# Window attention with a normalised feed-forward block: the largest weight is spread behind the first second product, in another bank, and GpSimd makes the weights' three low bits

## The chip, the core and the metric

The kernel runs on one core of one Trainium2 chip. A core has a matrix engine (TensorE, "PE" in the rows, its weight loads "PEld"), VectorE ("DVE"), ScalarE ("ACT"), GpSimd ("POOL") and a sync engine ("SP") whose queue issues every DMA of this kernel. Matmuls write into banks of PSUM; the other tiles lie in SBUF. The metric is the device time of one execution in microseconds (us); lower is better.

## The reference

Eight batches of 576 tokens with eight heads of 64 go through attention with a window of 64 keys, and the 4608 tokens of 512 numbers that come out go through a feed-forward block. Cut to what matters:

```python
scores = where(0 <= row - col < 64, (q @ k.T) / 8, -1e6)   # per batch and head
x = softmax(scores) @ v                      # 4608 x 512, heads side by side
h = x @ w_in                                 # first product, 512 -> 1024
e = exp(h - max(h)); sm = e / (sum(e) + 1e-9)
solu = h * sm
ln = (solu - mean(solu)) / sqrt(var(solu) + 1e-6) * g_ln
return ln @ w_out                            # second product, 1024 -> 512
```

The two weights come as 64-bit floats; the kernel turns them into 32-bit floats on the chip.

## The kernel before

**Tiles.** The 4608 tokens are 36 tiles of 128. Tile t is scored (`pS`, L491), its softmax rows `sS` are exponentiated on ScalarE (L528) and divided by their sums (`rec`, L540, then L544), turned (bank `t`, copied out as `PT`, L603) and multiplied with the values (`pX`, L622). The result `xH` (and from tile 3 on its rest `xL`) goes through the first product into `pH` (L650 for tiles 0 to 2, in full 32-bit; L661 from tile 3 on, three passes over split weights). `moe_norm` reads `pH` twice on VectorE (the maximum, L676, and the product with the exponentials, L681) and leaves the normalised rows `e` (L700). `pH` has one buffer, so the first product of a tile waits for L681 of the tile before.

**The second product.** It runs three tiles behind. Tile 0 is turned on TensorE (L756), multiplied with the gains into `yT` (ScalarE L764 for columns 0 to 3, VectorE L765 for 4 to 7) and multiplied in full 32-bit with the weights as they are (`pO`, L784). From tile 1 on the rows are split into two 16-bit planes `pl`, written to memory (`yd`, L737), read back turned (`yT`, L740) and multiplied with the split weights `w_outH` and `w_outL` in three passes (L794).

**Weights.** Eight blocks of 1 MB: 0 to 3 are `w_in`, 4 to 7 `w_out`. Of each, `raw` holds 1024 pairs (low word, high word) on a partition. ScalarE takes the magnitude of the high word (L353), VectorE clamps it (L355), shifts it (L358), puts sign and top bit back (L360) and adds the top three bits of the low word (L362). For blocks 4 to 7 the clamp also leaves each partition's largest value in `bound`.

**The largest weight.** `out_scale` turns `bound` into one scale for the split weights: small VectorE steps (L376 to L387) make a diagonal tile, one matmul with ones (L389) spreads it over all partitions, L391 takes the maximum, and L392 to L398 make the gains `gs_sb`, after which L425, L426 and L428 split `w_out`. The matmul writes into `pO_filler`, which shares its one PSUM buffer with the second product's `pO`; filler matmuls that only keep TensorE busy (L901) write there too. So L784 of tile 0 can't start before L391 has read.

**The order.** Every step is entered into a plan with an engine and a cost; the plan sorts all of them, and each engine runs its own list in that order and waits where it has to. `PLACES` says where tiles 2 to 5 are attended, `HOMES` which engine does a movable step, `RINGS` how many buffers a tile name has, `SCALED` in which round `out_scale` is entered.

Of the kernel before, what the change touches and what calls it, by code (L numbers as in the profile page):

```python
# [45 lines left out]
HOMES = {
    ("scale", 0, 0): "POOL", ("scale", 0, 1): "POOL", ("scale", 1, 0): "POOL", ("scale", 1, 1): "ACT",
    ("scale", 3, 0): "DVE", ("scale", 3, 1): "DVE", ("scale", 4, 0): "ACT", ("scale", 4, 1): "DVE",
    ("scale", 5, 0): "ACT", ("scale", 6, 1): "DVE", ("scale", 7, 1): "DVE", ("scale", 8, 0): "DVE",
    ("scale", 9, 0): "DVE", ("scale", 10, 0): "ACT",  # L50
    ("PT", 1, 0): "DVE", ("PT", 1, 1): "DVE", ("PT", 3, 0): "DVE", ("PT", 4, 1): "ACT", ("PT", 5, 1): "ACT",
    ("PT", 6, 1): "ACT",
    ("join", 4, 0): "DVE", ("join", 5, 1): "ACT", ("join", 7, 0): "ACT", ("join", 7, 1): "ACT",
    ("soft", 8, 0): "ACT", ("soft", 10, 0): "DVE",
    ("norm", 0, 0): "DVE", ("norm", 0, 1): "DVE", ("norm", 2, 0): "DVE", ("norm", 2, 1): "DVE",
    ("norm", 3, 0): "DVE",
    ("high planes", 1, 0): "DVE", ("high planes", 1, 1): "DVE", ("high planes", 2, 1): "DVE",
    ("high planes", 4, 0): "DVE", ("high planes", 6, 0): "DVE", ("high planes", 6, 1): "DVE",
    ("planes", 1, 1): "DVE", ("planes", 3, 1): "POOL", ("planes", 4, 0): "POOL", ("planes", 7, 0): "POOL",
    ("planes", 8, 0): "POOL",  # L60
    ("high", 0, 0): "POOL", ("high", 2, 0): "POOL", ("high", 2, 1): "POOL", ("high", 7, 0): "DVE",
    ("high", 7, 1): "POOL",
    ("split", 0, 1): "POOL", ("split", 2, 0): "POOL", ("split", 2, 1): "POOL", ("split", 3, 0): "POOL",
# [150 lines left out]
def tile_window_attention_solu_moe(  # L214
# [117 lines left out]
    def weight_block(i, src):  # L332
# [333 lines left out]
    def moe_norm(t):  # L666
# [284 lines left out]
```

## Time and profile before

| | us |
|---|---|
| median of 3 runs | 529.0 (528.93 to 529.11) |
| the profiled execution | 529.3 |
| its span, first to last instruction | 527.5 |
| TensorE busy in the span | 509.1 (97%) |
| VectorE, ScalarE, GpSimd busy | 363.5, 336.5, 256.4 |

The page counts a matmul as busy also where it stands at a lower clock, so the 97% is not 97% of the peak. All times in rows are from the span's start. A row of a timeline is: start, length, engine, line, operation, what it writes and reads, sizes, how many. Several instructions in a row are merged, so a length over many is that of all of them. "PEclk" is the granted TensorE clock: 1.00 is 2.4 GHz, 0.50 is 1.2 GHz.

### The profile page before, as it was taken

The page shows a single profiled execution, that of the slowest core. Times are in us where ns is not written, and L with a number is a line of the kernel's source. Part 1 is how long each engine was busy: PE and PEld are TensorE (multiplying, and loading weights), DVE is VectorE, ACT ScalarE, POOL GpSimd, SP SyncE. Part 2 cuts the span into 40 slices and gives each one's busy share as a digit, 9 for nine tenths or more (in the row PEclk, how much of TensorE's full clock was granted, in tenths as well). Part 3 has the DMA queues.
Part 4 walks back from the last instruction along what each step waited for, and adds up shares of the span by engine and source line. Part 5 has one row for each costly group of instructions (what it writes and reads, how often), then busy time and mean ns, then how long its engine had stood idle before and what let it go on. Part 6 is the DMA issues. An engine that isn't in the chain of part 4 may idle for free.

```text
span 527.5 us, 11422 instructions
## 1 busy us (share of the span) xinstructions
PE 509.1 (97%) x4238; PEld 339.3 (64%) x4238; DVE 363.5 (69%) x695; ACT 336.5 (64%) x968; POOL 256.4 (49%) x452
## 2 busy tenths in 40 slices
PE   8699985999999999999999999999999999999997
PEld 8566662676666666666666666666666666666653
DVE  4789996677677777777777777777777777745230
ACT  5458761778786666666666666666666666674240
POOL 5625551054466555555555555555555555562110
PEclk9799996999999999999999999999999999999999
DMA  8982243146899999999999899999999999699301
GB/s 347 418 315 92 68 132 108 49 147 217 250 251 251 262 251 247 260 258 251 248 250 250 245 252 264 267 252 252 248 246 231 264 248 260 190 236 206 101 24 56
DMA packets 157447, 115.56 MB, mean 219 GB/s; under 512 B 129872, under 2 KB 130128, under 8 KB 156880
## 3 DMA queue, kind: packets, MB, share of 16 engines
q1 hardware_dynamic: 157392, 114.84, 80.1%
q8 instruction: 33, 0.54, 0.4%
q14 instruction: 22, 0.18, 0.1%
HBM read 41.42 MB, written 41.42 MB: 157 GB/s over the span
## 4 chain that ended last, share of the span: by engine, by line
PE 89%; DVE 8%; POOL 1%; ACT 1%; issue 0%; POOLq 0%; ACTq 0%; DVEq 0%
PE pO L794 34%; PE pH L661 33%; PE pX L622 7%; PE pS L491 6%; PE pH L650 3%; PE pO L784 2%; PE pO_filler L901 1%; POOL sS L544 1%; PE pX L794 1%; PE t L598 1%; DVE w L360 1%; DVE w L362 1%; DVE mst L676 1%; DVE e L681 1%; DVE sS L544 1%; DVE w L355 1%
## 5 line engine op out<-in xcount | busy, mean ns | idle before, releaser
L794 PE MATMUL pO<-w_outH,yT 128*128 128x512 f16 x544 | 167.7, 380 | 0.0
L794 PEld LDWEIGHTS <-yT 128*128 128x128 f16 x840 | 79.6, 98 | 96.6 <-issue 5.1
L544 POOL TENSOR_SCALAR sS<-sS,rec 128x128 f32<-128x128 f32 x244 | 101.2, 436 | 83.2 <-DVE rec L540 51.7
L661 PE MATMUL pH<-w_inH,xH 128*128 128x512 f32 x264 | 110.4, 418 | 0.1
L528 ACT ACTIVATE sS<-sS,nmx 128x128 f32<-128x128 f32 x264 | 102.0, 389 | 7.5 <-DVE nmx L505 4.6
L661 PE MATMUL pH<-w_inH,xL 128*128 128x512 f32 x264 | 103.5, 392 | 0.8 <-DVE xL L633 0.8
L794 PE MATMUL pO<-w_outL,yT 128*128 128x512 f16 x272 | 103.1, 379 | 0.0
L661 PE MATMUL pH<-w,xH 128*128 128x512 f32 x264 | 101.6, 389 | 0.0
L676 DVE TENSOR_REDUCE mst<-pH 128x1 f32<-128x1024 f32 x36 | 44.1, 1224 | 60.6 <-PE pH L661 59.5
L731 DVE TENSOR_TENSOR pl<-e,pl 128x512 f16<-128x512 f32 x61 | 80.1, 1314 | 4.9 <-ACT pl L728 4.7
L694 POOL TENSOR_TENSOR mst<-mst,neghalf 128x1 f32<-128x1 f32 x36 | 20.4, 567 | 124.6 <-DVE mst L692 124.6
L805 ACT ACTIVATE ot<-pO,bound 128x512 f32<-128x512 f32 x34 | 23.4, 688 | 81.7 <-PE pO L794 72.6
L700 POOL TENSOR_SCALAR e<-e,mst 128x512 f32<-128x512 f32 x67 | 52.0, 783 | 20.7 <-DVE mst L695 20.2
L678 ACT ACTIVATE e<-pH,mst 128x1024 f32<-128x1024 f32 x36 | 40.2, 1117 | 29.4 <-DVE mst L676 28.4
L661 PEld LDWEIGHTS pH<-w_inH,xH 128*128 128x128 f32 x264 | 49.7, 188 | 13.0 <-issue 0.7
L661 PEld LDWEIGHTS pH<-w_inH,xL 128*128 128x128 f32 x264 | 49.4, 187 | 12.5 <-DVE xL L633 1.0
L661 PEld LDWEIGHTS pH<-w,xH 128*128 128x128 f32 x264 | 49.6, 188 | 10.5 <-issue 0.2
L564 POOL COPY raw<-sS 128x1024 uint16<-128x1024 uint16 x54 | 55.2, 1052 | 0.1
L687 ACT ACTIVATE pl<-e,mst 128x1024 bf16<-128x1024 f32 x36 | 41.4, 1149 | 15.8 <-DVE mst L684 14.3
L528 ACT ACTIVATION_READ_ACCUMULATOR sS<-sS,nmx 128x1 f32 x264 | 49.8, 189 | 0.0
L681 DVE CUSTOM_DVE_ANT_0 e<-pH,e 128x1024 f32<-128x1024 f32 x36 | 43.8, 1215 | 2.5 <-ACT e L678 2.5
L728 ACT CAST pl<-e 128x512 f16<-128x512 f32 x60 | 36.9, 617 | 5.3 <-POOL e L700 3.8
(117 smaller groups left out, 703.4 us busy)
## 6 DMA issues: line engine op xcount, KB each, us to landing
qk<-qk SPq DMA_DIRECT2D x36, 640.0 KB, 6.2
yd<-pl SPq DMA_DIRECT2D x33, 512.0 KB, 5.8
pd<-raw SPq DMA_DIRECT2D x28, 512.0 KB, 7.4
v<-vS SPq DMA_DIRECT2D x36, 256.0 KB, 4.2
y<-ot SPq DMA_DIRECT2D x35, 256.0 KB, 6.9
raw<-w_in SPq DMA_DIRECT2D x4, 1024.0 KB, 10.6
raw<-w_out SPq DMA_DIRECT2D x4, 1024.0 KB, 8.7
yT<-yd SPq DMA_TRANSPOSE x33, 5.3
```

Of the source, the lines that this page charges most:

```text
L528: plan.op("ACT", 580, lambda h=h: nc.scalar.activation(SS(t)[:, h], PS(t)[:, h // NPAIR, h % NPAIR] if t in MASKED else SS(t)[:, h], AF.Ex ...
L544: SS(t)[:, h], SS(t)[:, h], rec()[:, h:h + 1]) if e == "ACT" else units[e].tensor_scalar(
L564: plan.op(e, {"POOL": 1050, "ACT": 1000, "DVE": 700}[e], lambda x=x, e=e: copy_on(e)(PP(t)[:, :, 4 * x:4 * x + 4].rearrange("p k h n -> p ...
L622: nc.tensor.matmul(PX(t)[r * D:(r + 1) * D, p, ks], (V if half else VX)(t)[:, h * D:(h + 1) * D], PT(t)[:, r * NPAIR + p, ks], start=True, ...
L661: plan.op("PE", 233, lambda n=n, c=c, x=x, w=w: nc.tensor.matmul(PH(t)[:, hs], x(t)[:, c], w(c, h), start=(n == 0), stop=(n == len(passes) ...
L676: plan.op("DVE", 1230, lambda: nc.vector.tensor_reduce(nmax(), PH(t), axis=AX.X, op=ALU.max, negate=True), [("pH", t)], [key(0)])
L678: plan.op("ACT", 1320, lambda: nc.scalar.activation(E(t), PH(t), AF.Exp, bias=nmax(), scale=1.0, accum_out=se()), [("pH", t), key(0)], H2 ...
L681: plan.op("DVE", 1310, lambda: nc.vector.tensor_tensor_reduce(E(t), PH(t), E(t), scale=1.0, scalar=0.0, op0=ALU.mult, op1=ALU.add, accum_o ...
L687: plan.op("ACT", 1330, lambda: nc.scalar.activation(PL(t)[:, 0].bitcast(BF16), E(t), AF.Square, bias=nmean(), scale=1.0, accum_out=ss()), ...
L700: plan.op(e, {"POOL": 820, "DVE": 400}[e], lambda h=h, hs=hs, e=e: units[e].tensor_scalar(E(t)[:, hs], E(t)[:, hs], nmean(), kk(), ALU.add ...
L731: plan.op(e, {"POOL": 1450, "DVE": 690}[e], lambda hs=hs, e=e: units[e].tensor_sub(PL(t)[:, 1, hs], E(t)[:, hs], PL(t)[:, 0, hs]), [("e", ...
L794: plan.op("PE", 216, lambda f=f, i=i, x=x, k=k, y=y, w=w: nc.tensor.matmul(PO(), Y(t, y)[:, f], w(i, x), start=(f == k == 0), stop=(f == N ...
```

## The change

Parts, in the order of the diff:

- **Low bits.** ScalarE's magnitude is scaled by 2^-48, so the masks of L358 and L360 are not needed. A new step makes the three low bits of a block in place in `raw`: on GpSimd for seven blocks (a multiply and an add over 128x1024, read as unsigned integers), on VectorE for block 4. VectorE then has, for each block, the clamp and two two-input steps; the separate shift is gone, and the first two-input step waits for the new one.
- **`out_scale`.** Its matmul writes into a buffer of the transposes' bank `t`. It is entered after `moe_out` of round 3 and not before it, so it stands behind the second product of tile 0. One of its small steps goes.
- **First tile's rows** get a buffer `yF` of their own.
- **Square of `moe_norm`** writes into a tile `unread`, and no longer into the planes `pl` of its tile.
- **Tables.** Tile 4 is attended one place later, `PLANES` is 3, and `HOMES` puts other steps on other engines, among them four of tile 0's scalings on VectorE and most of the planes of tiles 2 to 5 on GpSimd.

```diff
+SHIFT = 2.0 ** -48
+LOW = 2.0 ** -29 * (1 - 2.0 ** -12)
-PLACES = {2: (0, 0), 3: (0, 2), 4: (1, 2), 5: (2, 2)}
+PLACES = {2: (0, 0), 3: (0, 2), 4: (1, 3), 5: (2, 2)}
-PLANES = 2
+PLANES = 3
 HOMES = {
-    ("scale", 0, 0): "POOL", ("scale", 0, 1): "POOL", ("scale", 1, 0): "POOL", ("scale", 1, 1): "ACT",
+    ("scale", 0, 1): "POOL", ("scale", 1, 0): "POOL", ("scale", 1, 1): "ACT", ("scale", 3, 0): "DVE",
...
+    ("low bits", 4, 0): "DVE",
...
-SCALED = 3
+SCALED = (3, 1)
...
+    unread = const.tile([P, DFF], BF16, name="unread")
...
-        plan.op("ACT", 1090, lambda: nc.scalar.activation(tf(), hi().bitcast(F32), AF.Abs), [R], [W])
+        plan.op("ACT", 1090, lambda: nc.scalar.activation(
+            tf(), hi().bitcast(F32), AF.Abs, scale=SHIFT), [R], [W])
+        e = home("low bits", i, 0, "POOL")
+        plan.op(e, {"POOL": 1900, "DVE": 700}[e], lambda: nc.gpsimd.tensor_scalar(
+            lo(), lo().bitcast(U32), LOW, 0.0018 - 0.5, ALU.mult, ALU.add) if e == "POOL" else nc.vector.tensor_scalar(
+            lo(), lo(), 29, 0, ALU.logical_shift_right, ALU.bitwise_or), [], [R])
...
-            tf(), tf(), EXP_HI, EXP_LO, ALU.min, ALU.max, accum_out=most), [W],
+            tf(), tf(), EXP_HI * SHIFT, EXP_LO * SHIFT, ALU.min, ALU.max, accum_out=most), [W],
-        plan.op("DVE", 700, lambda: nc.vector.tensor_scalar(
-            t(), t(), 0x07FFFFFF, 3, ALU.bitwise_and, ALU.logical_shift_left), [W], [W])
         plan.op("DVE", 1240, lambda: nc.vector.scalar_tensor_tensor(
-            t(), hi(), -0x40000000, t(), ALU.bitwise_and, ALU.bitwise_or), [R, W], [W])
+            t(), t(), 3, lo(), ALU.logical_shift_left, ALU.bitwise_or), [R, W], [W])
         plan.op("DVE", 1240, lambda: nc.vector.scalar_tensor_tensor(
-            t(), lo(), 29, t(), ALU.logical_shift_right, ALU.bitwise_or), [R, W], [W])
+            t(), hi(), -0x80000000, t(), ALU.bitwise_and, ALU.bitwise_or), [R, W], [W])
...
         def pM():
-            return T("pO", "filler", [P, DM], pool=ps_o)[:, P:2 * P]
+            return T("t", "most", [P, 4, P], pool=ps_t)[:, 0]
...
-            PL(t)[:, 0].bitcast(BF16), E(t), AF.Square, bias=nmean(), scale=1.0, accum_out=ss()),
-            H2 + [key(4)], [key(3), ("pl", t, 0), ("pl", t, 1)], lat=300)
+            unread, E(t), AF.Square, bias=nmean(), scale=1.0, accum_out=ss()),
+            H2 + [key(4)], [key(3)], lat=300)
...
-        return T("yT", t, [P, NF, P])
+        return T("yF" if t < PLAIN_OUT else "yT", t, [P, NF, P])
...
-            if t == SCALED:
+            if (t, 0) == SCALED:
                 out_scale()
...
             on(moe_out, t - BEHIND)
+            if (t, 1) == SCALED:
+                out_scale()
```

On TensorE, around the second product of tile 0 (`t_3` is the turning of tile 0's rows, `pS_6` the scores of tile 6, `pO_0` the second product, `pH_4` the first product of tile 4; the rows of `pX_4` are left out). Before:

```order
L756 MATMUL t_3_870<-ident_81,e_0_467 128x128 x4
L389 MATMUL pO_filler_173<-diag_123,ones_120 128x128
...
L901 MATMUL pO_filler_173<-ident_81 128x128 x4
L491 MATMUL pS_6_914<-qk_6_465 64x128 x16
L784 MATMUL pO_0_944<-w_4_510,yT_0_906 128x512 x2
L784 MATMUL pO_0_944<-w_5_521,yT_0_906 128x512 x2
L784 MATMUL pO_0_944<-w_6_639,yT_0_906 128x512 x2
L784 MATMUL pO_0_944<-w_7_648,yT_0_906 128x512 x2
L661 MATMUL pH_4_980<-w_inH_114,xH_4_942 128x512
```

And of the change:

```order
L764 MATMUL t_3_841<-ident_81,e_0_464 128x128 x4
...
L911 MATMUL pO_filler_174<-ident_81 128x128
L499 MATMUL pS_6_882<-qk_6_462 64x128 x16
L792 MATMUL pO_0_913<-w_4_509,yF_0_869 128x512 x2
L792 MATMUL pO_0_913<-w_5_516,yF_0_869 128x512 x2
L792 MATMUL pO_0_913<-w_6_621,yF_0_869 128x512 x2
L792 MATMUL pO_0_913<-w_7_633,yF_0_869 128x512 x2
L397 MATMUL t_most_954<-diag_124,ones_120 128x128
L669 MATMUL pH_4_957<-w_inH_114,xH_4_928 128x512
```

The spreading matmul stood ahead of `pO_0`, in its bank; now it stands behind it, in a bank of the transposes.

On VectorE at the same place (`w_6` and `w_7` are the last two weight blocks, `mst_3` and `e_3` the maximum and the exponentials' product of tile 3, `yT_0` or `yF_0` tile 0's turned rows, columns 4 to 7). Before:

```order
L358 TENSOR_SCALAR w_7_648<-w_7_648 128x1024
L360 SCALAR_TENSOR_TENSOR w_6_639<-raw_6_381,w_6_639 128x1024
L676 TENSOR_REDUCE mst_3_902<-pH_3_780 128x1
L362 SCALAR_TENSOR_TENSOR w_6_639<-raw_6_381,w_6_639 128x1024
L360 SCALAR_TENSOR_TENSOR w_7_648<-raw_7_412,w_7_648 128x1024
L765 TENSOR_SCALAR yT_0_906<-t_3_870,g_sb_117 128x128
L362 SCALAR_TENSOR_TENSOR w_7_648<-raw_7_412,w_7_648 128x1024
L765 TENSOR_SCALAR yT_0_906<-t_3_870,g_sb_117 128x128 x2
L681 ISA e_3_934,mst_3_902<-pH_3_780,e_3_934 128x1024
...
L519 SCALAR_TENSOR_TENSOR sS_6_960<-pS_6_914,maskNone_99 128x1024
...
L391 TENSOR_REDUCE bound_122<-pO_filler_173 128x1
```

And of the change:

```order
L371 SCALAR_TENSOR_TENSOR w_6_621<-w_6_621,raw_6_378 128x1024
...
L373 SCALAR_TENSOR_TENSOR w_6_621<-raw_6_378,w_6_621 128x1024
...
L371 SCALAR_TENSOR_TENSOR w_7_633<-w_7_633,raw_7_411 128x1024
...
L373 SCALAR_TENSOR_TENSOR w_7_633<-raw_7_411,w_7_633 128x1024
...
L684 TENSOR_REDUCE mst_3_846<-pH_3_767 128x1
L773 TENSOR_SCALAR yF_0_869<-t_3_841,g_sb_117 128x128 x4
L389 TENSOR_REDUCE bound_122<-bound_122 128x1
...
L527 SCALAR_TENSOR_TENSOR sS_6_915<-pS_6_882,maskNone_99 128x1024
L532 TENSOR_REDUCE nmx_6_924<-sS_6_915 128x8
L689 ISA e_3_921,mst_3_846<-pH_3_767,e_3_921 128x1024
...
```

The two shifts are gone, tile 0's rows stand ahead of tile 3's product, and the whole of `out_scale`'s second half stands behind both.

On GpSimd near the start (`vx` are joined value rows, `sS_0` to `sS_2` the scalings of tiles 0 to 2). Before:

```order
L458 COPY vx_0_221<-v_0_159 64x512 x2
L458 COPY vx_1_226<-v_0_159 64x512
L544 TENSOR_SCALAR sS_0_202<-sS_0_202,rec_0_271 128x128 x8
L458 COPY vx_1_226<-v_1_169 64x512
L458 COPY vx_2_361<-v_1_169 64x512
L458 COPY vx_2_361<-v_2_198 64x512
L544 TENSOR_SCALAR sS_1_287<-sS_1_287,rec_1_403 128x128 x4
```

And of the change:

```order
L466 COPY vx_0_222<-v_0_160 64x512
L364 TENSOR_SCALAR raw_0_158<-raw_0_158 128x1024
L552 TENSOR_SCALAR sS_0_203<-sS_0_203,rec_0_268 128x128 x4
L364 TENSOR_SCALAR raw_1_164<-raw_1_164 128x1024
L364 TENSOR_SCALAR raw_2_166<-raw_2_166 128x1024
L466 COPY vx_2_354<-v_1_170 64x512
L364 TENSOR_SCALAR raw_3_168<-raw_3_168 128x1024
L466 COPY vx_2_354<-v_2_199 64x512
L552 TENSOR_SCALAR sS_1_321<-sS_1_321,rec_1_401 128x128 x4
```

Four low-bit steps stand in GpSimd's list where four scalings and three copies stood. Those of blocks 5, 6 and 7 stand further down, behind the scalings of tile 2 and of tile 3. On SP the write of the first result tile (`y<-ot_0`) now stands one place ahead of the read of tile 1's turned rows (`yT_1`), where it stood behind those of tiles 1 and 2.

## Rows read from the trace of the kernel before

**Rows 1.** Waits of TensorE, 0 to 125 us: total, times, longest.

```profile
PE pO L784 <- DVE bound L391: 7.7, 1, 7.7
PE t L598 <- POOL sS L544: 4.1, 6, 1.5
PE pH L661 <- DVE xL L633: 0.8, 1, 0.8
```

**Rows 2.** Stretches: busy of PE, PEld, DVE, ACT, POOL; PEclk; DMA share; GB/s.

```profile
48.00:60.00 12.00, 12.00 (x104) 7.41 (x100) 12.00 (x33) 10.59 (x29) 5.15 (x7) 1.00 0.25 79
77.50:85.20 7.70, 0.03 (x4) 0.00 (x0) 7.70 (x15) 2.10 (x5) 0.05 (x1) 0.68 0.96 237
85.20:90.00 4.80, 4.75 (x6) 2.19 (x7) 3.13 (x10) 1.12 (x4) 2.36 (x5) 0.50 0.01 2
110.00:200.00 90.00, 90.00 (x792) 61.09 (x792) 65.80 (x129) 67.97 (x202) 50.90 (x85) 1.00 0.89 235
200.00:460.00 260.00, 260.00 (x2251) 174.01 (x2250) 185.61 (x322) 177.04 (x520) 143.96 (x262) 1.00 0.98 251
```

**Rows 3.** Chain that ended last, in order of time: start, length.

```profile
30.99 3.63 PE pH L650 x8
...
95.00 2.75 PE pH L661 x12
...
103.49 5.29 PE pO L794 x24
```

**Rows 4.** Timeline of TensorE.

```profile
49.95 1.83 PE L901 MATMUL pO_filler<-ident 128*128 128x128 f32 x14
51.74 7.11 PE L650 MATMUL pH<-w,xH 128*128 128x512 f32 x16
...
73.94 0.39 PE L389 MATMUL pO_filler<-diag,ones 128*128 128x128 f32 x2
...
76.42 1.10 PE L491 MATMUL pS<-qk 64*64 64x128 f32 x32
85.25 9.75 PE L784 MATMUL pO<-w,yT 128*128 128x512 f32 x16 [7.72 <-DVE bound L391]
```

**Rows 5.** Timeline of VectorE.

```profile
25.79 1.11 DVE L358 TENSOR_SCALAR w<-w 128x1024 int32<-128x1024 int32 x1
...
28.47 1.22 DVE L362 SCALAR_TENSOR_TENSOR w<-raw,w 128x1024 int32<-128x1024 int32 x1
...
34.66 1.23 DVE L676 TENSOR_REDUCE mst<-pH 128x1 f32<-128x1024 f32 x1 [1.12 <-PE pH L650]
...
73.90 1.28 DVE L358 TENSOR_SCALAR w<-w 128x1024 int32<-128x1024 int32 x2
75.11 1.21 DVE L360 SCALAR_TENSOR_TENSOR w<-raw,w 128x1024 int32<-128x1024 int32 x1
...
79.91 1.21 DVE L362 SCALAR_TENSOR_TENSOR w<-raw,w 128x1024 int32<-128x1024 int32 x1
...
82.70 0.34 DVE L765 TENSOR_SCALAR yT<-t,g_sb 128x128 f32<-128x128 f32 x1
```

**Rows 6.** Timeline of GpSimd.

```profile
14.10 7.74 POOL L544 TENSOR_SCALAR sS<-sS,rec 128x128 f32<-128x128 f32 x8 [3.94 <-DVE rec L540]
...
25.48 1.88 POOL L458 COPY vx<-v 64x512 f32<-64x512 f32 x2 [3.10 <-PE pX L622]
30.00 1.43 POOL L544 TENSOR_SCALAR sS<-sS,rec 128x128 f32<-128x128 f32 x4 [2.64 <-DVE rec L540]
```

**Rows 7.** GpSimd by line and shape, 0 to 90 us: busy us, mean ns.

```profile
L421 POOL TENSOR_TENSOR w<-w,w_inH 128x512 fp32r<-128x512 f32 x5 | 6.8, 1377 | 2.0 <-PE t L598 1.9
L700 POOL TENSOR_SCALAR e<-e,mst 128x512 f32<-128x512 f32 x2 | 1.8, 897 | 0.1
L426 POOL TENSOR_SCALAR w_outH<-w,gs_sb 128x512 f16<-128x512 f32 x1 | 1.0, 988 | 0.3 <-DVE bound L398 0.3
```

**Rows 8.** DMA issues, 60 to 125 us: KB each, median us from issue to landing.

```profile
yT<-yd SPq DMA_TRANSPOSE x3, 5.3
```

More of the change, by code (lines that the diff above doesn't have):

```diff
@@ L42 @@
 JOINS = 8
-PLANES = 2
+PLANES = 3
 HOMES = {
-    ("scale", 0, 0): "POOL", ("scale", 0, 1): "POOL", ("scale", 1, 0): "POOL", ("scale", 1, 1): "ACT",
[L48 to L59, printed above, removed]
+    ("scale", 0, 1): "POOL", ("scale", 1, 0): "POOL", ("scale", 1, 1): "ACT", ("scale", 3, 0): "DVE",
+    ("scale", 4, 0): "ACT", ("scale", 4, 1): "DVE", ("scale", 5, 0): "ACT", ("scale", 5, 1): "ACT",
+    ("scale", 6, 0): "ACT", ("scale", 6, 1): "ACT", ("scale", 8, 0): "DVE", ("scale", 8, 1): "DVE",
+    ("scale", 10, 0): "ACT",
+    ("PT", 0, 0): "DVE", ("PT", 1, 0): "DVE", ("PT", 1, 1): "DVE", ("PT", 2, 0): "DVE", ("PT", 4, 1): "ACT",
+    ("PT", 5, 1): "ACT", ("PT", 6, 0): "DVE", ("PT", 7, 1): "ACT",
+    ("join", 0, 0): "ACT", ("join", 1, 0): "ACT", ("join", 1, 1): "ACT", ("join", 3, 0): "ACT",
+    ("join", 3, 1): "ACT", ("join", 4, 0): "ACT", ("join", 4, 1): "ACT",
+    ("soft", 9, 0): "DVE", ("soft", 9, 1): "DVE", ("soft", 10, 0): "ACT", ("soft", 10, 1): "ACT",
+    ("norm", 0, 1): "DVE", ("norm", 2, 0): "DVE", ("norm", 2, 1): "DVE", ("norm", 3, 1): "DVE",
+    ("norm", 4, 0): "DVE", ("norm", 5, 1): "DVE",
+    ("high planes", 2, 0): "DVE", ("high planes", 2, 1): "POOL", ("high planes", 3, 0): "POOL",
+    ("high planes", 3, 1): "POOL", ("high planes", 4, 0): "POOL", ("high planes", 4, 1): "POOL",
+    ("high planes", 5, 0): "POOL", ("high planes", 5, 1): "POOL", ("high planes", 6, 0): "DVE",
+    ("high planes", 6, 1): "DVE",
+    ("planes", 2, 1): "DVE", ("planes", 5, 0): "POOL", ("planes", 5, 1): "POOL", ("planes", 7, 0): "POOL",
@@ L60 @@
     ("planes", 8, 0): "POOL",
[L61 to L63 removed]
+    ("high", 1, 0): "DVE", ("high", 2, 0): "POOL", ("high", 2, 1): "POOL", ("high", 3, 0): "POOL",
+    ("high", 4, 1): "POOL", ("high", 7, 0): "POOL",
+    ("low bits", 4, 0): "DVE",
+    ("split", 0, 0): "POOL", ("split", 0, 1): "POOL", ("split", 2, 0): "POOL", ("split", 3, 0): "POOL",
@@ L389, in out_scale @@
         plan.op("PE", 280, lambda: nc.tensor.matmul(pM(), ones, diag, start=True, stop=True),
-                [("diag",)], [("all",)])
-        small(lambda: nc.vector.tensor_reduce(b, pM(), axis=AX.X, op=ALU.max), [("all",)], [("b",)], 200)
+                [("diag",)], [("t", "most")])
+        small(lambda: nc.vector.tensor_reduce(b, pM(), axis=AX.X, op=ALU.max), [("t", "most")], [("b",)], 200)
         small(lambda: nc.vector.tensor_scalar(
@@ L457, in join @@
             e = home("join", t, x, "POOL" if t < JOINS else "ACT")
-            plan.op(e, {"POOL": 620, "ACT": 590, "DVE": 400}[e], lambda e=e, rows=rows, u=u: copy_on(e)(
+            plan.op(e, {"POOL": 700, "ACT": 590, "DVE": 400}[e], lambda e=e, rows=rows, u=u: copy_on(e)(
                 VX(t)[rows], V(u)[rows]), [("v", u)], [("vx", t, x)])
@@ L786, in moe_out @@
                     start=(f == 0), stop=(f == NF - 1)),
-                    [("yT", t, f), ("w", NC + f // 2)], [bank])
+                    [("yF", t, f), ("w", NC + f // 2)], [bank])
         for f in range(NF if t >= PLAIN_OUT else 0):
```

10 lines of the change are left out of this document (4 added, 6 removed), and 2 rows, old and new, of the table RINGS.

## The prediction

> **What bounds the kernel now.** I read the waits of TensorE first, then the stretches, then the chain and the timelines. TensorE has one long wait in the whole run: 7.7 us ahead of L784, the second product of tile 0, until L391 has read the bank [rows 1]. The stretches show what the wait costs beyond itself: from 77.5 to 85.2 TensorE is idle, and behind it the granted clock is 0.50, that is 1.2 GHz [rows 2]. From 110 to 460 us TensorE is busy in every microsecond at 1.00 [rows 2]; the chain is TensorE alone from 85.25 up to the last result. So whatever brings the start of tile 1's second product (103.49, [rows 3]) forward brings the end forward by as much, provided that nothing new stops TensorE behind it. All that this change can give lies in the first 103 us. I cut them at three places: the end of tile 0's first product (30.99 + 3.63 = 34.62, [rows 3]), the start of L784 (85.25), and 103.49.
>
> **Up to 34.62: weights and first tile.** Before, block 3 is ready at 28.47 + 1.22 = 29.69 [rows 5], and TensorE starts on the second half of that product at 30.99, behind the scores of tile 2, so the weights just don't matter there. What leads up to it is GpSimd's eight scalings of tile 0, which take 7.74 us where four later ones take 1.43 [rows 6], 0.97 against 0.36 each. The change gives four of them to VectorE, and puts four low-bit steps into GpSimd's list, three of them behind the scalings and ahead of block 3.
>
> No row shows a low-bit step. It is one GpSimd pass with one input over 128x1024. Twice the passes over 128x512 gives 1.8 (L700, 0.897), 2.0 (L426, 0.988, with a type conversion as here) and 2.75 (L421, two inputs) [rows 7]. I take 2.0, since L426 is the same operation with a conversion, and keep 1.8 and 2.75 for the range; that it is much longer is a rival below.
>
> These steps also stand in VectorE's way. While two copies ran on GpSimd from 25.48 to 27.36 [rows 6], a shift took 1.11 on VectorE at 25.79, against 0.64 each for the pair at 73.90 [rows 5]; and GpSimd's scalings were stretched as said. So I let the two engines take turns from about 13.7, when tile 0's sums are ready (GpSimd's scalings start at 14.10 before). VectorE then has three clamps at 0.64 and six two-input steps at 1.22 (9.2) and four scalings of some 0.3 (1.2); GpSimd has four scalings (1.43), three low-bit steps (6.0) and a copy (0.9). Together 18.7, less about 1.2 in which VectorE reads PSUM: block 3 is ready at 13.7 + 17.5 = 31.2, 1.5 later than before. Only the last quarter of the product needs it (3.63 / 2 = 1.8 for one block at full clock): it ends at 33.0 at full clock, and at 34.8 if that last block runs at half clock because TensorE stood idle ahead of it. I take **no change, 34.6**; the bounds are -2 (1.8 per step, some overlap) and +3.5 (2.75 per step is 2.25 more, raw_0's step ahead of tile 0's sums 0.75 more, and both blocks at half clock).
>
> A rule of the Trainium skill bears on this (SBUF — State Buffer, § Who interferes with whom): VectorE instructions with two SBUF inputs, or in the two-port mode, and GpSimd instructions share one pair of ports under an exclusive lock, and the loser is blocked for the whole instruction. The trace agrees with the direction (1.11 against 0.64). By it taking turns is the rule and not a worst case, and the 31.2 would stand; without it both lists would run side by side and block 3 would be ready 1.5 or more ahead of 29.7. It speaks against this part of the change.
>
> **From 34.62 to L784.** Before, TensorE needs 42.9 us up to the end of tile 6's scores (76.42 + 1.10 = 77.52, [rows 4]) and then waits 7.7. The wait goes: the spreading matmul stands behind the product and in another bank. In the 42.9 us the list held 26 fillers and now holds 21, at 0.26 each (1.79 for seven, 49.95 to 51.74, [rows 4]): -1.3. The spreading matmul goes from here: -0.3 (73.94, [rows 4]). Three low-bit steps (blocks 5, 6 and 7, 6 us of GpSimd) come in. VectorE loses eight shifts of 0.64 over the whole run (5.1) [rows 5] and gets one low-bit step (0.64 to 1.22), so I charge 1.0 for the steps' collisions; bounds 0 and 3. Sum 42.3, so L784 starts at **76.9** and not at 85.25: -8.35.
>
> What is late next? Its second half needs columns 4 to 7 of tile 0 and blocks 6 and 7. Were VectorE exactly as late as before, block 7 would be there at 79.91 + 1.21 = 81.1 and the last column at 83.04 [rows 5]. A product of 7.1 us begun at 76.9 asks for block 7 at 82.2 and the last column at 83.1. So an unchanged VectorE would just do, and this one has less ahead of it: the second pass over tile 3 (L681) now stands behind the columns.
>
> **L784 itself.** It takes 9.75 before, most of it at 0.50; the same sixteen matmuls over tile 2 take 7.11 at 1.00 [rows 2, 4]. With the idle 7.7 gone the clock has no reason to fall: -2.65, bounds -2.65 and 0. It ends at 84.0, where it ended at 95.0.
>
> **From there to tile 1's second product.** Before 103.49 - 95.00 = 8.49 [rows 3], none of it waiting. The spreading matmul comes in: +0.3. The gains and the split of w_out follow L784 as they did, since the splits on ScalarE waited for the result of tile 0 in both. New is SP's order: the write of tile 0's result stands ahead of the turned read of tile 1. That read is issued some 1.0 behind 84.0 and lands 5.3 later [rows 8], at 90.3, and TensorE wants it at 84.0 + 8.8 = 92.8: 2.5 to spare, if GpSimd, which now makes the planes, isn't late. I count tile 2, whose planes come behind the split weights on VectorE, the same. I charge 0.5, bounds 0 and 3.
>
> **Sum.** -8.35 - 2.65 + 0.3 + 0.5 = -10.2. What follows 103.49 costs the same: TensorE's list there is the same, and the moved planes and scalings of tiles 4 to 10 lie beside a TensorE that is never idle; if that cover fails it costs what the planes are late. The profiled execution took 529.3 (span 527.5 and 1.8 around it), so 519.1; it lies 0.3 above the median of 529.0, so the forecast for the median is **518.8**.
>
> **Rivals.**
> 1. *The wait moves to VectorE.* The low-bit steps block it for all of their 6 us, it comes to the last columns some 4 later than before, at 87, and TensorE stops inside L784; the clock falls again. L784 then ends near 89 instead of 84.0: 524. For it: VectorE is busy without a break from 48 to 60 [rows 2]. Against: the 5.1 us of shifts that it loses, and L681 moved behind. Chance 0.15.
> 2. *Tile 1's or tile 2's turned rows come late*, since most planes are now GpSimd's and the read is behind a write on SP: 2 to 3 us at each, 4 to 5 in all: 523.5. For it: only 2.5 to spare. Against: GpSimd was busy 5.15 of 12 us in the middle stretch [rows 2]. Chance 0.12.
> 3. *Slower than before: the low-bit steps starve the weights.* Were each stretched as tile 0's scalings were, 0.97 against 0.36, 2.0 would become 5.4; four of them lie ahead of block 3, each 3.4 longer: +13.6, so 529.3 - 10.2 + 13.6 = 532.7, 532.4 against the median. It decides from 10.2 / 4 = 2.6 more per step, 4.6 us each. For it: the stretched scalings are of the same stretch and engine [rows 6]. Against: VectorE waits for these very steps, and while it waits it takes nothing from GpSimd. Chance 0.06.
> 4. *No change worth having*, with the front 3.5 later, the collisions 3 and both turned tiles late: 528 to 529. Chance 0.03.
>
> **How the numbers follow.** The forecast has 0.64. Its own range is 518.8 - 3.9 (front -2, no collisions -1, no late tile -0.5, a rest of the 0.8 wait for xL gone [rows 1]) to + 3.5: 514.5 to 522.3. To leave out no more than 2 in 10 the upper end takes in rivals 1 and 2: 514.5 to 524.5. A difference of 0.2% (1.06 us) is about what a measurement of this kernel can tell from none. Faster by more: 0.91 (forecast, rivals 1 and 2). Within it: 0.03. Slower by more: 0.06 (rival 3).
>
> **What would show it.** Right: no wait ahead of the second product of tile 0, which starts near 77 and takes about 7.1 at 1.00; tile 1's second product near 93; TensorE without idle from there. The low-bit step shows its price in its own row, and the front in the end of tile 0's first product near 34.6. Wrong: a wait of TensorE at tile 0's second product for VectorE's columns (rival 1) or at tile 1's or 2's for a DMA (rival 2), low-bit steps over 4 us (rival 3), or a granted clock below 1.00 between 77 and 93.

## The result, and the profile after

| | before | after |
|---|---|---|
| median, us | 529.06 (528.93 to 529.16) | 516.74 (516.58 to 517.75) |
| the profiled execution, us | 529.3 | 516.58 |
| its span, us | 527.5 | 514.8 |
| TensorE busy | 509.1 (97%) | 503.9 (98%) |
| VectorE, ScalarE, GpSimd busy, us | 363.5, 336.5, 256.4 | 362.6, 338.9, 261.7 |

The ratio of after to before is 0.977, 95% interval 0.975 to 0.979: 12.3 us less. The forecast was 518.8, in a range of 514.5 to 524.5. VectorE is busy for about as long as before; what changed is where it is late.

The waits of TensorE in the kernel after, from 0 to 125 us (total, times, longest):

```profile
PE pH L669 <- DVE mst L689: 3.3, 1, 3.3
PE pO_filler L911 <- POOL ident masks.py:199: 1.5, 1, 1.5
PE pH L658 <- DVE w L373: 1.1, 2, 0.7
...
PE t L606 <- POOL sS L552: 0.3, 1, 0.3
```

The 7.7 us ahead of the second product of tile 0 [rows 1] are gone, and of the 4.1 us behind GpSimd's scalings 0.3 are left. New are 1.1 us inside tile 0's first product, for its weights, and 3.3 us ahead of L669: tile 3's first product waits until VectorE has read tile 2's. Stretches of the kernel after (columns as in [rows 2]):

```profile
48.00:60.00 12.00, 11.97 (x104) 7.34 (x102) 12.00 (x20) 7.72 (x24) 8.68 (x10) 1.00 0.36 126
60.00:72.00 12.00, 8.75 (x38) 7.09 (x39) 11.55 (x27) 9.16 (x30) 6.63 (x7) 0.86 0.09 23
74.90:82.10 7.20, 7.20 (x23) 3.37 (x19) 4.82 (x12) 4.83 (x16) 2.83 (x3) 1.00 0.56 200
200.00:460.00 260.00, 260.00 (x2223) 173.90 (x2222) 184.03 (x325) 178.96 (x523) 144.10 (x262) 1.00 0.96 248
```

The stretch in which the clock falls has moved from the second product of tile 0 to 60 to 72 us, behind that new wait. TensorE's timeline in the kernel after; the last rows are the second product of tile 0, the spreading matmul, and the first matmul of tile 1's second product:

```profile
25.31 1.98 PE L658 MATMUL pH<-w,xH 128*128 128x512 f32 x4 [0.74 <-DVE w L373]
27.70 1.98 PE L658 MATMUL pH<-w,xH 128*128 128x512 f32 x4 [0.41 <-DVE w L373]
...
63.25 0.76 PE L669 MATMUL pH<-w_inH,xH 128*128 128x512 f32 x1 [3.28 <-DVE mst L689]
...
74.91 7.13 PE L792 MATMUL pO<-w,yF 128*128 128x512 f32 x16
81.88 0.38 PE L397 MATMUL t_most<-diag,ones 128*128 128x128 f32 x2
...
90.70 0.39 PE L802 MATMUL pO<-w_outH,yT 128*128 128x512 f16 x1
```

The chain of waits in the kernel after, in order of time, around the new wait:

```profile
61.96 1.13 DVE e L689
...
63.25 4.64 PE pH L669 x12
67.89 0.87 PE t L606 x8
68.77 2.81 PE pH L669 x12
```

Twelve matmuls of the same shapes take 4.64 behind the wait and 2.81 in the product's second half: 1.8 us of lower clock (the granted clock is 0.66 from 63 to 68 us and 1.00 from 68 to 72). With the prediction's three cuts:

| stretch | before | predicted | after |
|---|---|---|---|
| to the end of tile 0's first product | 34.62 | 34.6 | 29.68 (27.70 + 1.98) |
| from there to the start of tile 0's second product | 50.63 | 42.3 | 45.23 |
| that product | 9.75 | 7.1 | 7.13 |
| from its end to tile 1's second product | 8.49 | 9.3 | 8.66 |
| the rest of the span | 424.0 | 424.0 | 424.1 |

The span came out 2.5 us below the forecast (514.8 for 517.3; the median 2.1): errors of -4.9 in the front, +2.9 in the middle and -0.6 behind it partly cancel. VectorE's and GpSimd's timelines of the kernel after, where the two meet (VectorE first):

```profile
13.65 0.90 DVE L552 TENSOR_SCALAR sS<-sS,rec 128x128 f32<-128x128 f32 x4
...
17.27 2.17 DVE L371 SCALAR_TENSOR_TENSOR w<-w,raw 128x1024 int32<-128x1024 int32 x1
...
26.42 1.22 DVE L373 SCALAR_TENSOR_TENSOR w<-raw,w 128x1024 int32<-128x1024 int32 x1
...
48.53 3.07 DVE L552 TENSOR_SCALAR sS<-sS,rec 128x128 f32<-128x128 f32 x4
...
52.41 2.12 DVE L373 SCALAR_TENSOR_TENSOR w<-raw,w 128x1024 int32<-128x1024 int32 x1
...
58.07 1.21 DVE L684 TENSOR_REDUCE mst<-pH 128x1 f32<-128x1024 f32 x1
...
60.49 0.88 DVE L552 TENSOR_SCALAR sS<-sS,rec 128x128 f32<-128x128 f32 x4
```

```profile
8.79 1.14 POOL L364 TENSOR_SCALAR raw<-raw 128x1024 int32<-128x1024 uint32 x1
13.35 2.13 POOL L552 TENSOR_SCALAR sS<-sS,rec 128x128 f32<-128x128 f32 x4 [3.42 <-ACT w L361]
15.56 2.80 POOL L364 TENSOR_SCALAR raw<-raw 128x1024 int32<-128x1024 uint32 x2
...
49.01 2.50 POOL L429 TENSOR_TENSOR w<-w,w_inH 128x512 fp32r<-128x512 f32 x2
...
52.16 3.42 POOL L364 TENSOR_SCALAR raw<-raw 128x1024 int32<-128x1024 uint32 x2
```

Against [rows 5, 6]: block 3 is ready at 27.64 and not at 29.69, four scalings on GpSimd take 2.13 and not 7.74 for eight. Where a GpSimd step of two SBUF inputs or a low-bit step runs, VectorE's step beside it takes up to 3.5 times its usual time (3.07 against 0.88, 2.12 against 1.22). It is not always VectorE that loses: at 13.65 its four scalings take 0.90, and GpSimd's four beside them 2.13, where four take 1.43 in [rows 6]. GpSimd by line, 0 to 90 us, answering [rows 7]:

```profile
L364 POOL TENSOR_SCALAR raw<-raw 128x1024 int32<-128x1024 uint32 x7 | 11.2, 1598 | 0.6
```

Answering [rows 8], the turned reads take a median of 5.1 and none is waited for.

### The profile page after: what moved, and what is told of

It is laid out like the page before. It is cut to its first block, busy times and chain, and to the rows that moved or that the text cites. A ratio compares the mean times of both kernels' runs of the same rounds, so it can differ in the third digit from the quotient of the medians.

```text
span 514.8 us, 11432 instructions
## 1 busy us (share of the span) xinstructions
PE 503.9 (98%) x4222; PEld 335.7 (65%) x4222; DVE 362.6 (70%) x677; ACT 338.9 (66%) x978; POOL 261.7 (51%) x459
## 4 chain that ended last, share of the span: by engine, by line
PE 90%; DVE 7%; DMA 1%; issue 1%; ACT 1%; DVEq 0%; ACTq 0%
PE pH L669 36%; PE pO L802 35%; PE pX L630 7%; PE pS L499 6%; PE pH L658 2%; DVE w L371 1%; PE pO L792 1%; DVE w L373 1%; DVE w L368 1%; PE pX L802 1%; DVE sS L552 1%; PE t L606 1%; DMA qk<-qk 1%; DVE nmx L520 1%; PE t L764 1%
## 5 line engine op out<-in xcount | busy, mean ns | idle before, releaser
L552 POOL TENSOR_SCALAR sS<-sS,rec 128x128 f32<-128x128 f32 x240 | 92.4, 406 | 69.1 <-DVE rec L548 64.8
L669 PE MATMUL pH<-w_inH,xH 128*128 128x512 f32 x264 | 111.0, 421 | 3.3 <-DVE mst L689 3.3
L669 PE MATMUL pH<-w_inH,xL 128*128 128x512 f32 x264 | 104.3, 395 | 0.0
L669 PE MATMUL pH<-w,xH 128*128 128x512 f32 x264 | 101.6, 389 | 0.0
L684 DVE TENSOR_REDUCE mst<-pH 128x1 f32<-128x1024 f32 x36 | 44.0, 1224 | 56.9 <-PE pH L669 55.8
L739 DVE TENSOR_TENSOR pl<-e,pl 128x512 f16<-128x512 f32 x59 | 78.2, 1328 | 3.4 <-ACT pl L736 3.3
L686 ACT ACTIVATE e<-pH,mst 128x1024 f32<-128x1024 f32 x36 | 40.1, 1114 | 32.4 <-DVE mst L684 30.5
L669 PEld LDWEIGHTS pH<-w_inH,xH 128*128 128x128 f32 x264 | 50.2, 190 | 16.1 <-ACT w_inH L427 3.4
L669 PEld LDWEIGHTS pH<-w_inH,xL 128*128 128x128 f32 x264 | 49.9, 189 | 11.9 <-DVE xL L641 0.3
L669 PEld LDWEIGHTS pH<-w,xH 128*128 128x128 f32 x264 | 49.7, 188 | 10.3
L572 POOL COPY raw<-sS 128x1024 uint16<-128x1024 uint16 x52 | 53.0, 1049 | 0.9 <-DVE sS L552 0.9
L695 ACT ACTIVATE unread<-e,mst 128x1024 bf16<-128x1024 f32 x36 | 41.3, 1149 | 16.5 <-DVE mst L693 11.9
L689 DVE CUSTOM_DVE_ANT_0 e<-pH,e 128x1024 f32<-128x1024 f32 x36 | 43.8, 1216 | 2.5 <-ACT e L686 2.5
L499 PE MATMUL pS<-qk 64*64 64x128 f32 x1152 | 39.8, 276 | 0.1
```

The lines of the kernel that those rows point to most:

```text
L499: nc.tensor.matmul(PS(t)[half * WIN:(half + 1) * WIN, r, p], q[rs, p, half * WIN:(half + 1) * WIN], keys, start=t not in MASKED, stop=t no ...
L552: SS(t)[:, h], SS(t)[:, h], rec()[:, h:h + 1]) if e == "ACT" else units[e].tensor_scalar(
L572: plan.op(e, {"POOL": 1050, "ACT": 1000, "DVE": 700}[e], lambda x=x, e=e: copy_on(e)(PP(t)[:, :, 4 * x:4 * x + 4].rearrange("p k h n -> p ...
L669: plan.op("PE", 233, lambda n=n, c=c, x=x, w=w: nc.tensor.matmul(PH(t)[:, hs], x(t)[:, c], w(c, h), start=(n == 0), stop=(n == len(passes) ...
L684: plan.op("DVE", 1230, lambda: nc.vector.tensor_reduce(nmax(), PH(t), axis=AX.X, op=ALU.max, negate=True), [("pH", t)], [key(0)])
L686: plan.op("ACT", 1320, lambda: nc.scalar.activation(E(t), PH(t), AF.Exp, bias=nmax(), scale=1.0, accum_out=se()), [("pH", t), key(0)], H2 ...
```

## The experiments

Ratios are to the kernel before in the same set of runs (its medians there: 529.7, 530.5, 530.0). The changed kernel's is 0.977. Of long table lines the diffs show only the entries that change.

**1. The bank alone.** The kernel before, with the spreading matmul in the bank `t` and behind the product.

```diff
-            return T("pO", "filler", [P, DM], pool=ps_o)[:, P:2 * P]
+            return T("t", "most", [P, 4, P], pool=ps_t)[:, 0]
...
             on(moe_out, t - BEHIND)
+            if t == SCALED:
+                out_scale()
```

> The kernel before, with only the largest weight's spreading moved: its matmul in a buffer of the transposes' bank and out_scale behind the second product of tile 0. Theory A (the wait at the bank and the low clock behind it are the gain): the second product of tile 0 starts right behind the scores of tile 6, near 78 instead of 85.25, waits at most about 1 us inside for VectorE's last column (83.0 in the kernel before), takes 7 to 8.5 us instead of 9.75, and the run takes 519 to 521. Rival B (the wait only changes its name, because VectorE is late for the columns and the last weight blocks unless it loses the shifts): the product starts early and stands still inside, the clock falls, and the run takes 525 to 528.

526.5, ratio 0.995 (0.993 to 0.996). TensorE, then ScalarE in this run:

```profile
81.89 9.70 PE L784 MATMUL pO<-w,yT 128*128 128x512 f32 x16 [3.85 <-ACT yT L764]
```

```profile
80.38 1.11 ACT L678 ACTIVATE e<-pH,mst 128x1024 f32<-128x1024 f32 x1 [2.74 <-DVE mst L676]
...
81.48 0.36 ACT L764 ACTIVATE yT<-t,g_sb 128x128 f32<-128x128 f32 x1
```

The wait got another name: ScalarE's fourth column of tile 0 stands behind tile 3's exponentials (L678), and these wait for VectorE's maximum. Rival B held. The move also re-sorted VectorE's list: that maximum (L676) begins at 79.07 here and at 76.24 in the kernel before, where the same column ends at 79.01, 1.5 behind the scores of tile 6. So part of the 3.85 is the new order.

**2. The changed kernel with the bank and the place of before.**

```diff
-            return T("t", "most", [P, 4, P], pool=ps_t)[:, 0]
+            return T("pO", "filler", [P, DM], pool=ps_o)[:, P:2 * P]
...
-SCALED = (3, 1)
+SCALED = (3, 0)
```

> The changed kernel with only the spreading put back: in the filler's bank and ahead of the second product of tile 0. Theory A: the wait for the maximum comes back in front of that product, 3 to 8 us, with the low clock behind it, and the run takes 522 to 527. Rival B: VectorE, without the shifts, reads the bank in time, the wait is under 2 us, and the run takes 517 to 519.

518.1, ratio 0.978 (0.976 to 0.980). VectorE in this run:

```profile
75.31 0.28 DVE L399 TENSOR_REDUCE bound<-pO_filler 128x1 f32<-128x128 f32 x1
```

It reads the bank at 75.31, and TensorE comes to the product at 76.18 and doesn't wait. Rival B held: with this VectorE list the bank kept causes no wait. That the product starts 1.3 us later than in the changed kernel comes from further ahead, where TensorE waits 4.08 and not 3.28:

```profile
64.05 0.77 PE L669 MATMUL pH<-w_inH,xH 128*128 128x512 f32 x1 [4.08 <-DVE mst L689]
```

**3. All eight low-bit steps on VectorE.**

```diff
-    ("low bits", 4, 0): "DVE",
+    ("low bits", 0, 0): "DVE", ("low bits", 1, 0): "DVE", ... ("low bits", 7, 0): "DVE",
```

> The changed kernel with all eight low-bit steps on VectorE and none on GpSimd. Theory A (VectorE's own time is short at the start; a step of 0.9 us there costs more than its collisions do from GpSimd): the end of tile 0's first product moves from 29.7 to 32 to 36 and the run takes 519 to 523. Rival C (the collisions of GpSimd's low-bit steps with VectorE are the larger cost, since VectorE lost about 3.4 us to them around 48 to 55): the wait ahead of tile 3's first product (3.3) shrinks under 1 us and the run takes 513 to 517.

521.2, ratio 0.983 (0.980 to 0.986): A held. The wait ahead of tile 3's first product is 2.1 (C had it under 1). The first product of tile 0 ends at 34.2 again:

```profile
30.47 3.70 PE L658 MATMUL pH<-w,xH 128*128 128x512 f32 x8
```

That product starts early here, at 17.5, but block 3 is ready only at 28.9, and the scores of tile 2, which end at 30.5, stand ahead of the second half.

**4. Low bits on GpSimd and the buffers, with tables, bank and place of before.**

```diff
-PLACES = {2: (0, 0), 3: (0, 2), 4: (1, 3), 5: (2, 2)}
+PLACES = {2: (0, 0), 3: (0, 2), 4: (1, 2), 5: (2, 2)}
-PLANES = 3
+PLANES = 2
...
```

> The changed kernel with the tables (homes, places, planes) and the spreading of the kernel before: what is left of the change is the low bits on GpSimd, the buffer for tile 0's rows and the square's own tile. Theory A: VectorE is 2 to 4 us shorter ahead of the maximum, the wait at the bank stays with 3 to 6 us, and the run takes 524 to 528. Rival B: the shifts were what held the product, the wait goes, and the run takes 517 to 520.

524.1, ratio 0.988 (0.984 to 0.993); its four runs spread from 520.4 to 526.0, and the profiled one took 522.8. The time is A's and the trace is not: nothing waits at the bank, as B had it. The waits of TensorE are 3.7 and 3.6 elsewhere. The first product of tile 0 starts at 25.6, behind eight GpSimd scalings that take 6.34, and ends at 33.9, so the tables are needed for the front:

```profile
PE t L602 <- POOL sS L548: 3.7, 4, 1.5
PE pX L626 <- DVE PT L607: 3.6, 1, 3.6
```

**5. Tile 3's four scalings from VectorE to GpSimd.**

```diff
-    ("scale", 3, 0): "DVE",
```

> The changed kernel with one entry of the table less: the four scalings of tile 3 that VectorE does (3.07 us at 48.53, against 0.88 for four others at 60.49) go to GpSimd, which then does all eight. Theory A (in the changed kernel VectorE loses some 2.2 us there to GpSimd's two-input splits at 49.01, so that tile 2's maximum and its exponentials' product come late, TensorE waits 3.3 ahead of tile 3's first product and its clock falls): the wait is under 1.5 us, tile 3's first product takes close to 2.8 and not 4.6 at its start, the second product of tile 0 starts near 71 and the time is 511.5 to 514.5. Rival B (the collisions only move, since the splits and low-bit steps on GpSimd stay and now stand behind eight scalings; or the second product then waits for VectorE's last blocks): a wait of 2.5 or more stays ahead of tile 3's first product or appears ahead of the second product of tile 0, and the time is 515.5 to 518.

516.0, ratio 0.972 (0.971 to 0.974). The time is rival B's, and so is the mechanism, though less of the wait stays than it had: 2.2 of the 3.3 us, where B had 2.5 or more. VectorE in this run:

```profile
54.71 1.23 DVE L684 TENSOR_REDUCE mst<-pH 128x1 f32<-128x1024 f32 x1
...
58.76 2.25 DVE L552 TENSOR_SCALAR sS<-sS,rec 128x128 f32<-128x128 f32 x4
60.93 1.21 DVE L689 CUSTOM_DVE_ANT_0 e<-pH,e 128x1024 f32<-128x1024 f32 x1
```

The maximum is taken 3.4 earlier than at 58.07, but the product that frees the bank (L689) stands behind splits and scalings that collide in their turn, and begins only 1.0 earlier than at 61.88.

**6. The front's table entries of before.**

```diff
-    ("scale", 0, 1): "POOL",
+    ("scale", 0, 0): "POOL", ("scale", 0, 1): "POOL",
-    ("PT", 0, 0): "DVE",
```

> The changed kernel with the front's table entries as before: all eight scalings of tile 0 on GpSimd, and tile 0's first turned half copied out by ScalarE; low-bit steps stay where they are. Theory A (the front's 4.9 us come from taking tile 0's scalings apart, which lets TensorE begin tile 0's first product at 19 and not at 26): the first product of tile 0 ends at 33 to 35 and the time is 519.5 to 522. Rival B (they come from the weights, whose low-bit step costs 1.14 to 2.0 on GpSimd and frees VectorE, so that block 3 is ready at 27.6): the first product ends at 29.5 to 31.5 and the time is 516 to 518.5.

520.9, ratio 0.983 (0.981 to 0.985). The front went B's way, the time A's. GpSimd, then TensorE in this run:

```profile
13.23 3.31 POOL L552 TENSOR_SCALAR sS<-sS,rec 128x128 f32<-128x128 f32 x8 [3.44 <-DVE rec L548]
```

```profile
27.39 3.70 PE L658 MATMUL pH<-w,xH 128*128 128x512 f32 x8 [0.38 <-DVE w L373]
...
67.48 0.76 PE L669 MATMUL pH<-w_inH,xH 128*128 128x512 f32 x1 [4.82 <-ACT unread L695]
```

The product ends at 31.1: only 1.4 of the 4.9 us hang on the scalings' place. The eight scalings take 3.31 where they took 7.74. VectorE's weight steps in that time:

```profile
13.91 0.73 DVE L368 TENSOR_SCALAR w<-w 128x1024 f32<-128x1024 f32 x1 [0.30 <-ACT w L361]
...
18.24 2.19 DVE L371 SCALAR_TENSOR_TENSOR w<-w,raw 128x1024 int32<-128x1024 int32 x1
```

Beside the scalings stands one clamp, and the next two-input step comes behind block 1's low bits; in the kernel before, seven weight steps of VectorE lay beside them. Most of the rest of the loss lies at tile 3's first product, where the wait is 4.8 and not 3.3.

**7. Without both new buffers.**

```diff
-        return T("yF" if t < PLAIN_OUT else "yT", t, [P, NF, P])
+        return T("yT", t, [P, NF, P])
...
-            unread, E(t), AF.Square, bias=nmean(), scale=1.0, accum_out=ss()),
+            PL(t)[:, 0].bitcast(BF16), E(t), AF.Square, bias=nmean(), scale=1.0, accum_out=ss()),
```

> The changed kernel without the two buffers: tile 0's rows again share the three buffers yT, and the square of the normalisation writes again into the planes of its tile, and so waits for them. Theory A (these two edits give nothing; the time went through VectorE, the tables and the bank): within 1 us of the changed kernel, 516 to 518. Rival B (the square's wait for a planes' buffer holds ScalarE and through it VectorE's rows): 518.5 to 522, with a new wait of TensorE at tile 1's or tile 2's second product or at the normalisation.

530.2, ratio 1.000 (0.999 to 1.001): the whole gain is gone, which neither theory had. The waits of TensorE:

```profile
PE pO L792 <- ACT yT L772: 9.6, 1, 9.6
PE pH L669 <- DVE mst L689: 2.8, 1, 2.8
```

Again it is ScalarE's fourth column, which here stands behind tile 3's exponentials and eight scalings that wait for VectorE:

```profile
83.42 2.45 ACT L551 ACTIVATE sS<-sS,rec 128x128 f32<-128x128 f32 x8 [4.79 <-DVE rec L548]
...
86.15 0.35 ACT L772 ACTIVATE yT<-t,g_sb 128x128 f32<-128x128 f32 x1
```

**8. Tile 3's four scalings to ScalarE.**

```diff
-    ("scale", 3, 0): "DVE",
+    ("scale", 3, 0): "ACT",
```

> As the run on tile 3's scalings, but the four go to ScalarE, whose four scalings later take some 1.4 us (0.40 and 0.98 at 60.55). Theory A (it is VectorE's lost time that makes tile 3's first product late): the wait ahead of it is under 1.5 us and the time is 511.5 to 514.5, like the run with GpSimd. Rival B: the four stand ahead of tile 4's exponentials or of the last magnitudes on ScalarE and only move the wait: 515.5 to 518.

515.2, ratio 0.972 (0.970 to 0.974). The waits of TensorE:

```profile
PE pX L630 <- DMA raw<-pd: 1.2, 1, 1.2
...
PE pH L669 <- DVE mst L689: 0.6, 1, 0.6
```

A's mechanism held, the time lies between the two. The second product of tile 0 starts at 72.75 and tile 1's at 88.56, 2.1 earlier; but between 125 and 200 us TensorE waits 1.2 for a turned read, with the DMA engines at a share of 1.00:

```profile
125.00:200.00 75.00, 73.68 (x656) 49.32 (x655) 48.66 (x94) 52.65 (x151) 42.59 (x77) 1.00 1.00 251
```

The changed kernel has 1.02 there and no such wait, so a full DMA stream isn't a sufficient cause; what makes that read late stays open. The profiled execution is the slowest of the four (516.5, the others 515.1 to 515.2), so the wait may be of that execution alone. By the times this kernel is 1.6 faster than the changed kernel; that one did not run beside it, and experiment 12, which should equal it, had 0.974, so the advantage is likely and not shown.

**9. The rows' buffer alone.** The kernel before with `yF`.

```diff
-        return T("yT", t, [P, NF, P])
+        return T("yF" if t < PLAIN_OUT else "yT", t, [P, NF, P])
...
```

> The kernel before with one edit of the change alone: tile 0's turned rows get a buffer of their own. The plan then puts ScalarE's four columns of tile 0 together, where the fourth stood behind tile 3's exponentials. Theory A (by itself the buffer frees nothing on TensorE's path, since the spreading matmul still holds the bank until VectorE has taken the maximum): TensorE waits 6 us or more ahead of the second product of tile 0 for that maximum, and the time is 526 to 530. Rival B (the buffer carries most of the change's gain): the wait is under 3 us and the time 517 to 523.

532.8, ratio 1.005 (1.004 to 1.007): slower by 0.5%. A's wait is there (6.96), and the time is above both ranges; its profile also shows new waits of 1.9 ahead of tile 3's first product and of 2.1 for a turned read behind 125 us. VectorE reads the bank here:

```profile
85.05 0.23 DVE L391 TENSOR_REDUCE bound<-pO_filler 128x1 f32<-128x128 f32 x1
```

**10. Bank and rows' buffer together,** weights and tables as before (the edits of 1 and 9).

> The kernel before with two edits of the change: the spreading matmul behind the second product and in the transposes' bank, and tile 0's rows in their own buffer; weights and tables as before. Theory A (with the bank free and ScalarE's four columns together, a VectorE that is as loaded as before does keep up, as the prediction said, and what the bank move alone lacked was this place on ScalarE): no wait over 1 us ahead of the second product of tile 0, which starts at 76 to 79 and takes about 7.1; the time is 518 to 522. Rival B (VectorE, with its shifts, is late in either order, and the wait goes to its last columns or blocks, or ahead of tile 3's first product): a wait of 3 us or more for VectorE, a lowered clock again, 523 to 527.

523.5, ratio 0.988 (0.986 to 0.989). TensorE in this run:

```profile
67.89 0.80 PE L661 MATMUL pH<-w_inH,xL 128*128 128x512 f32 x1 [1.79 <-DVE xL L633]
...
79.22 7.13 PE L784 MATMUL pO<-w,yF 128*128 128x512 f32 x16
```

Both were half right. No wait is left at the second product of tile 0 with VectorE's list as heavy as before (A), but 0.9 and 1.8 us now stand ahead of and in tile 3's first product, at a clock of 0.86 from 60 to 72 us (B), and the time is B's. Further on TensorE waits 0.8 at the spreading matmul and 1.2 for turned rows.

**11 and 12. Each buffer taken from the changed kernel by itself,** by the lines of experiment 7.

> The changed kernel with tile 0's rows back among the three buffers yT, and nothing else. Without both buffers it lost all of its gain. Theory A (it is this buffer: without it the plan puts ScalarE's fourth column of tile 0 behind tile 3's exponentials and three scalings of tile 6, which wait for VectorE): a wait of 5 us or more ahead of the second product of tile 0 for ScalarE's column, 524 to 531. Rival B (it is the square's tile): 516 to 518.5, no such wait.

527.0, ratio 0.995 (0.994 to 0.997). The wait has its cause but not its size: 3.0 for ScalarE's column. The second product starts at 83.44, 8.5 later than in the changed kernel: behind tile 3's first product TensorE also waits 1.2 and 0.9 for GpSimd, and its list has more ahead of the second product. That product then takes 8.83 and not 7.13.

> The changed kernel with the square written into the planes of its tile again, and nothing else. Theory A (the other buffer carries it; ScalarE's list keeps the four columns together): 516 to 518.5, no wait ahead of the second product of tile 0. Rival B (it is the square's tile, whose writing holds a planes' buffer and so the split rows of tiles 1 and 2): 522 to 531, with a wait of TensorE at tile 0's or tile 1's second product.

516.3, ratio 0.974 (0.973 to 0.976), no wait at the product: A. With the rows' buffer in place the square's tile gives nothing. Without that buffer it seems to give 0.5% (7 has 1.000, 11 has 0.995, in different sets of runs); why is open.

## Why the prediction came out right, point by point

**The total: right, and in part by luck.** The front missed its own bounds, the middle came near the end of its bounds on the other side, and the two errors offset each other. Also, the range's lower end of 514.5 is 0.4 below its own sum (518.8 - 3.9 = 514.9); the result lies inside either way.

**The wait at the bank and the clock behind it: right in size, wrong in the reason.** 7.7 us of waiting and 2.6 of lower clock went. But the bank alone was not what held the product. The bank without the buffer gives 0.5% (1), the buffer without the bank costs 0.5% (9), both give 1.2% (10); and once VectorE is relieved, the bank may stay as it was (2). Two late paths held it, and both lead back to VectorE: its own reading of the bank, and ScalarE's fourth column, queued behind exponentials that wait for VectorE. With either path left in the list of before the product still waits (1, 9). "So an unchanged VectorE would just do" overlooked that second path; it is true at this product only with the rows' buffer, by which the plan puts the four columns together (10). The prediction gave that buffer no price; it decides 1.8% (11). Why the plan sorts so was read from its lists, and not tested; no run changes one edge and keeps the order of the lists, so how much of each step is load and how much is order stays open.

**The front: the step that was mis-sized.** "No change", bounds -2 and +3.5; measured -4.9. A low-bit step was taken as 2.0 and costs 1.14 where nothing stretches it and 1.6 in the mean. With 1.14 the prediction's own sum, in which the two engines take turns, has block 3 ready at 28.6 and not at 31.2; it was ready at 27.64. The forecast then leaned to half clock for the last quarter, 3.4 behind block 3, and it took 2.0. So about 2.6 of the miss is the price of the step, 1.0 overlap and 1.4 the clock. Against the kernel before, two paths had to get shorter: GpSimd's scalings, which decide where the product starts, and the weights, which decide where it ends. Low bits on GpSimd without the tables leave the scalings slow, 0.79 each, and the end at 33.9 (4); the rest of the change with those steps on VectorE leaves the weights late and the end at 34.2 (3). The argument against rival 3, that VectorE stands behind these steps and so takes little from GpSimd, held: where it does, GpSimd's scalings, too, run at 0.41 each and not at 0.97 (6).

A rule of the Trainium skill was weighed there (SBUF — State Buffer, § Who interferes with whom): VectorE instructions with two SBUF inputs and GpSimd instructions that read SBUF share a pair of ports under an exclusive lock. Single rows of the trace agree: 2.17 and 2.12 against 1.22 for a step with two inputs. The whole front doesn't decide between taking turns and running side by side: the prediction expected 31.2 by the one and 28.2 or less by the other, and 27.64 looks like the other, but with the step's measured price turns give 28.6.

**The middle: 45.2 for 42.3.** Collisions were charged 1.0. They cost more, and in a place that counts: VectorE loses 2.2 in L552 and 0.9 in L373 between 48 and 55, comes to tile 2's product late, and TensorE waits 3.3 and then runs 1.8 at the lower clock. Without the charge the prediction had 41.3; with 3.3 and 1.8, and less the 0.8 of the wait for xL that is gone, it is 45.6, against 45.2 measured. This is rival 1's mechanism at another place, the first product of tile 3. This loss isn't independent of the front. In the kernel before, where VectorE is through with tile 2's product just ahead of TensorE, the rows are (from the chain and from TensorE's timeline):

```profile
63.38 1.13 DVE e L681
```

```profile
64.80 0.47 PE L661 MATMUL pH<-w_inH,xH 128*128 128x512 f32 x1
```

In the changed kernel VectorE is through at 63.09 and not at 64.51, 1.4 earlier, while TensorE could have begun at 59.97 (63.25 - 3.28) and not at 64.80, 4.8 earlier. So VectorE isn't later than before; it follows only part of the front's gain. An earlier front is not the whole cause, as waits of 2.1 and 4.8 stand there also in 3 and 6, where the front ends later. Experiments 5 and 8 show that it isn't the collision alone but what the list puts between the maximum (L684) and the product (L689).

**Rivals 2 and 3** didn't come: the turned rows are in time (8.66 for 9.3), and no low-bit step took over 2.04.

## What to carry to other kernels

A wait that ends on one engine's instruction shows who was last, not who is late: before moving the thing waited for, look at what the next-latest input stands behind in its queue, on every engine that feeds the instruction. Where a plan sorts the lists, an edit with no cost of its own can re-sort them, so each edit is priced with its list and tried alone and together.

## What the runs showed that was not expected

- A pass of GpSimd over 128x1024 integers at a stride of two words (one input, a multiply and an add with conversion) takes 1.14 us where nothing stretches it; two passes over 128x512 had taken 1.8 to 2.0 [rows 7].
- Four scalings of 128x128 took 0.88 us on VectorE and 3.07 beside GpSimd's two-input steps; eight on GpSimd took 3.31 with one weight step of VectorE beside them and 7.74 with seven.
- Low bits on GpSimd and the tables, either of which without the other (4, 3) leaves the first product's end nearly where it was (33.9 and 34.2 against 34.6), together bring it to 29.7.
